# Transposing normed tokens by DMA instead of TensorE in a planned two-layer kernel

## Chip, cores, metric

One core of a Trainium2 chip.

## The reference, cut

Two layers, each a memory-augmented recurrent transformer block followed by a gated feed-forward network (FFN). 2048 tokens, width 512, 32 heads of 128, segments of 32 tokens with 8 memory tokens carried from one segment to the next.

```python
for s in range(n_seg):                          # 64 segments, in sequence
    h = concat([mem, x[:, s*32:(s+1)*32]], 1)   # 8 + 32 tokens
    q, k, v = h@Wq, h@Wk, h@Wv                  # 32 heads of 128
    p = softmax(where(mask, q@k.T * scale, -1e9))
    o = (p @ v) @ Wo
    mem = o[:, :8]; outs.append(o[:, 8:])
x = x + A(layernorm(x)); x = x + B(layernorm(x))   # B: sigmoid(x@Wg) * (x@Wu) @ Wd
x = x + A(layernorm(x)); x = x + B(layernorm(x))
```

The chain through `mem` is what forbids doing the segments side by side. The kernel therefore runs the two layers interleaved, six steps apart, in 70 steps of one segment each.

## The kernel before

The kernel doesn't write its instructions in program order. It adds *tasks* with reads, writes and assumed durations to a planner. The planner simulates the engines 24 times, forwards and backwards, keeps the order with the shortest forecast, and then emits the instructions in that order. Each engine's order is fixed from then on.

```python
    LAT = {"PE": 205.0, "DVE": 110.0, "ACT": 128.0, "POOL": 40.0, "SP": 4000.0}
    TO_PE = 32.0
    WAIT = 65.0                       # ns that the planner adds to a VectorE/ScalarE task with several waits
...
    def plan(self, rounds=24):        # keeps the best of 24 forecasts
```

A block is four segments, 128 tokens. Its tokens are normalized into `xn` (128 tokens x 512 features) and transposed, four 128x128 squares, into a PSUM bank. From there they are copied to `hT`, where the projections read them:

```python
    def layernorm_T(self, xb, xkey, rw=slice(0, P)):
        ...
        xn = pl.buf(self.xnp)
        ...
        pl.add("DVE", 340, lambda: nc.vector.tensor_scalar(out=xn[rw, :], in0=xb, scalar1=ln[rw, 6:7], scalar2=ln[rw, 9:10], op0=ALU.subtract, op1=ALU.mult),
               r=xkeys + [lk], w=[xn])
        B = pl.buf(self.bank, "bg")
        ...
        def tr():
            for c in range(DC):
                nc.tensor.transpose(out=pst()[:, c, rw], in_=xn[rw, c * P:(c + 1) * P], identity=self.ident[rw, rw])

        pl.add("PE", DC * mm_ns(rw.stop - rw.start), tr, r=[xn], w=[B])
        return pst, B
```

`pre1(b)` does this for the tokens of a first-layer block, four steps before their use. `v_fill`/`ln_x` does it for blocks 6, 9, 12, 15 once more, for rows that fill up a value pass. Meanwhile GpSimd keeps loading FFN weights, 256 KB a load, over and over (219, 219 and 218 loads for the three matrices, by the page). `last_weights` loads those of the last FFN, from SyncE or GpSimd as the planner likes.

## Time and profile before

| | before |
|---|---|
| time, median of 4 | 1878.2 us (1876.1 to 1882.9; 1879.8 was the median of the 3 known when predicting) |
| span of the profiled run, granted clock | 1874.4 us, 0.997 |
| TensorE busy | 98% |
| DMA traffic | 273.8 MB, of which GpSimd's weight loads 181.9 MB |

The prediction below shows the profile's lines. The list of DMA queues (queue and kind: packets, MB, share of 16 engines):

```profile
q0 software_dynamic: 59184, 181.87, 33.3%
q1 hardware_dynamic: 73918, 85.92, 16.1%
q8 instruction: 323, 5.29, 1.2%
```

q0 holds GpSimd's weight loads, q1 what SyncE issues. q8 carries *instructions*: 323 packets of 16 KB. In the trace TensorE runs 82762 instructions (matmuls, weight loads and a few others), 323.3 times 256: from these counts I estimate one packet for 256 of them, at 64 bytes each. So TensorE's program itself arrives by DMA, on a queue that the page lists beside those of the data, with 1.2% of the span of the core's 16 DMA engines.

### The profile page before, as it was taken

How to read it: one execution, taken by the hardware profiler on the slowest of the kernel's cores; microseconds unless marked ns; L12 is line 12 of the kernel's file. 1: busy time of each engine (PE TensorE's matmuls, PEld its weight loads, DVE VectorE, ACT ScalarE, POOL GpSimd, SP SyncE). 2: the span in 40 equal slices, each digit the busy share in tenths (PEclk: the TensorE clock that was granted, in tenths of full speed). 3: DMA queues.
4: the chain of work that ended last, by engine and by line, in shares of the span. 5: the costliest groups of instructions: out<-in, count | busy, mean ns of one | idle time of the engine just before them, and what ended most of it. 6: DMA issues, size and time to landing. Idle time of an engine off the chain costs nothing.

```text
span 1874.4 us, 94356 instructions
## 1 busy us (share of the span) xinstructions
PE 1835.2 (98%) x41250; PEld 1579.0 (84%) x41250; DVE 1281.1 (68%) x4167; ACT 1137.5 (61%) x2690; POOL 576.2 (31%) x822
## 2 busy tenths in 40 slices
PE   7999899999999999999999999999999999999998
PEld 3578788888889898989889898989889898988787
DVE  5466567776777667776676677666777677766564
ACT  5655566666666666566666666666666666665553
POOL 5413012232423232333323333233323232323321
PEclk9999999999999999999999999999999999999999
DMA  9734234554645554555545544555545454555535
GB/s 353 249 99 114 77 86 119 152 155 128 182 125 152 150 142 122 153 151 148 166 121 148 157 142 132 140 153 151 160 126 155 125 155 127 147 144 151 152 90 143
DMA packets 133516, 273.83 MB, mean 146 GB/s; under 512 B 29254, under 2 KB 64846, under 8 KB 133102
## 3 DMA queue, kind: packets, MB, share of 16 engines
q0 software_dynamic: 59184, 181.87, 33.3%
q1 hardware_dynamic: 73918, 85.92, 16.1%
q8 instruction: 323, 5.29, 1.2%
q14 instruction: 91, 0.75, 0.1%
HBM read 222.04 MB, written 27.26 MB: 133 GB/s over the span
## 4 chain that ended last, share of the span: by engine, by line
PE 94%; DMA 1%; ACT 1%; DVE 1%; issue 1%; POOL 1%; SPq 0%; ACTq 0%; POOLq 0%; DVEq 0%
PE bank L707 32%; PE bank L808 16%; PE bank L907 11%; PE bank L570 9%; PE bank L678 7%; PE bank L931 5%; PE bank L721 5%; PE bank L780 4%; PE bank L791 4%; PE bank L540 1%; ACT otsb L999 1%; DMA vsb<-sst 0%; PE bank L875 0%; DMA wd<-in_B_w_down_dram 0%; DMA wv_sb<-in_A_Wv_dram 0%
## 5 line engine op out<-in xcount | busy, mean ns | idle before, releaser
L707 PE MATMUL bank<-hT,wq_sb 128*128 128x80 bf16 (+1 forms) x8960 | 625.8, 198 | 5.6 <-issue 2.7
L707 PE MATMUL bank<-hT,wk_sb 128*128 128x80 bf16 (+1 forms) x8960 | 624.3, 198 | 2.1 <-issue 2.1
L999 ACT CAST qku<-bank 128x480 bf16<-128x480 f32 (+3 forms) x770 | 394.0, 512 | 267.3 <-PE bank L707 256.1
L707 PEld LDWEIGHTS <-wq_sb 128*128 128x128 bf16 x8960 | 459.1, 100 | 31.3 <-issue 12.0
L707 PEld LDWEIGHTS <-wk_sb 128*128 128x128 bf16 x8960 | 451.7, 99 | 1.2 <-issue 1.2
L734 DVE TENSOR_TENSOR st<-bank,maskb 80x240 f32<-80x240 f32 (+1 forms) x732 | 268.8, 369 | 231.8 <-PE bank L721 225.0
L808 PE MATMUL bank<-otsb,wo_sb 128*128 128x80 bf16 (+1 forms) x8960 | 372.0, 198 | 6.1 <-ACT otsb L999 5.4
L808 PEld LDWEIGHTS <-wo_sb 128*128 128x128 bf16 x8960 | 339.5, 99 | 21.7 <-issue 9.4
L899 POOL DMA_DIRECT2D wg<-in_B_w_gate_dram x217 | 165.0, 760 | 501.2 <-PE bank L907 425.9
L999 ACT CAST otsb<-bank 128x480 bf16<-128x480 f32 (+3 forms) x420 | 200.6, 486 | 77.3 <-PE bank L791 61.9
L925 POOL DMA_DIRECT2D wd<-in_B_w_down_dram x217 | 153.7, 710 | 251.6 <-PE bank L791 99.5
L763 DVE TENSOR_TENSOR pb<-st,rz 80x480 bf16<-80x480 f32 x348 | 205.9, 592 | 3.5
L744 ACT ACTIVATE st<-st 80x240 f32<-80x240 f32 (+3 forms) x420 | 159.9, 382 | 67.0 <-DVE st L741 65.4
L999 ACT CAST ptsb<-bank 128x480 bf16<-128x480 f32 (+3 forms) x315 | 155.8, 501 | 65.6 <-PE bank L780 63.2
L530 POOL TENSOR_TENSOR lns<-lns,negh 128x1 f32<-128x1 f32 (+1 forms) x79 | 45.3, 576 | 451.1 <-DVE lns L529 336.7
L746 DVE TENSOR_REDUCE sm<-st 80x6 f32<-80x240 f32 (+3 forms) x420 | 151.8, 363 | 43.7 <-ACT st L744 41.8
L721 PE MATMUL bank<-qku 128*80 128x80 bf16 (+1 forms) x2240 | 177.4, 202 | 0.0
L907 PE MATMUL bank<-xnT,wg 128*128 128x128 bf16 (+2 forms) x1784 | 171.8, 219 | 1.9 <-DMA wd<-in_B_w_down_dram 1.3
L907 PE MATMUL bank<-xnT,wu 128*128 128x128 bf16 (+2 forms) x1784 | 171.2, 218 | 0.4 <-issue 0.4
L721 PEld LDWEIGHTS <-qku 128*80 128x80 bf16 (+1 forms) x2240 | 130.4, 117 | 44.5 <-issue 10.6
L900 POOL DMA_DIRECT2D wu<-in_B_w_up_dram x217 | 162.5, 749 | 4.6 <-PE bank L707 2.0
L741 DVE TENSOR_TENSOR st<-st,mx 80x240 f32<-80x240 f32 (+3 forms) x420 | 155.8, 371 | 3.9
(99 smaller groups left out, 2499.9 us busy)
## 6 DMA issues: line engine op xcount, KB each, us to landing
wg<-in_B_w_gate_dram POOLq DMA_DIRECT2D x219, 256.0 KB, 4.3
wd<-in_B_w_down_dram POOLq DMA_DIRECT2D x219, 256.0 KB, 5.3
wu<-in_B_w_up_dram POOLq DMA_DIRECT2D x218, 256.0 KB, 4.8
vsb<-scr SPq DMA_DIRECT2D x512, 48.0 KB
vsb<-sst SPq DMA_DIRECT2D x280, 64.0 KB
scr<-vst SPq DMA_DIRECT2D x128, 96.0 KB
wv_sb<-in_A_Wv_dram SPq DMA_DIRECT2D x4, 1024.0 KB
wq_sb<-in_A_Wq_dram SPq DMA_DIRECT2D x5, 768.0 KB
```

The costliest lines, as they stand in the source:

```text
L570: nc.tensor.matmul(B[:, :], lhsT=tile[:, c, :], rhs=self.wv[:, c, cs], start=(c == 0), stop=(c == DC - 1))
L707: nc.tensor.matmul(o_ap, lhsT=W[:, c, h * P:(h + 1) * P], rhs=mv(c), start=(c == 0), stop=(c == DC - 1))
L721: nc.tensor.matmul(s_all(SB)[pr, uh - h0 + i, :], lhsT=qku[:, i, 0, 0:ncol], rhs=qku[:, i, 1, 0:ncol], start=True, stop=True)
L734: pl.add("DVE", dve_ns(n, True), lambda gsz=gsz, hs=hs, st=st, SB=SB, pj_=pj_, npj_=npj_, mk=mk, idx=idx: nc.vector.tensor_tensor(out=st[p ...
L741: pl.add("DVE", dve_ns(n), lambda gsz=gsz, hs=hs, st=st, mx=mx: nc.vector.tensor_tensor(out=st[pr, hs], in0=st[pr, hs], in1=mx[pr, hs].uns ...
L744: pl.add("ACT", act_ns(n), lambda hs=hs, st=st: nc.scalar.activation(out=st[pr, hs], in_=st[pr, hs], func=ACTF.Exp, scale=self.scale), r=s ...
L763: nc.vector.tensor_tensor(out=o, in0=st[pr, hs].unsqueeze(1).to_broadcast([npart, 2, gsz, L]), in1=rz[pr, :, 0:gsz].unsqueeze(3).to_broadc ...
L808: nc.tensor.matmul(WB[:, c * ncol:(c + 1) * ncol], lhsT=self.wo[:, h, c * P:(c + 1) * P], rhs=otsb[:, hl, 0:ncol], start=(h == 0 and c == ...
L899: pl.add("POOL", 760, lambda wg=wg, fs=fs: nc.gpsimd.dma_start(out=wg[:], in_=self.wgv[:, :, fs]), r=[("wo", self.H - 1)], w=[gk] + bt, la ...
L900: pl.add("POOL", 760, lambda wu=wu, fs=fs: nc.gpsimd.dma_start(out=wu[:], in_=self.wuv[:, :, fs]), r=[("wo", self.H - 1)], w=[uk] + bt, la ...
L907: nc.tensor.matmul(gu[:, 2 * i + k, 0:n], lhsT=W[:, c, i * P:(i + 1) * P], rhs=xnT[:, c, rw], start=(c == 0), stop=(c == DC - 1))
L999: nc.scalar.copy(out=dst, in_=src)
```

## The change

Intent: take 18 of the 79 groups of transposes off TensorE, which is busy 98% of the time, and let the transposing DMA do them, as the DMA engines are about half busy outside the boot; and keep the last FFN's weight loads out of SyncE's queue. The diff, cut (the copies `write_hT_x` and `take_v` only learn to wait for a list of keys):

```diff
-    def layernorm_T(self, xb, xkey, rw=slice(0, P)):
+    def layernorm_T(self, xb, xkey, rw=slice(0, P), by_dma=False):
 ...
-        xn = pl.buf(self.xnp)
+        xn, xk = (self.xp, "xp") if by_dma else (pl.buf(self.xnp),) * 2
 ...
-               r=xkeys + [lk], w=[xn])
+               r=xkeys + [lk], w=[xk])
+        if by_dma:
+            q = self.nxt("xvt", 2)
+            tile_, keys = self.xvf[q], [("xvf", q, g) for g in range(4)]
+            pl.add("SP", 1250, lambda: nc.sync.dma_start_transpose(out=tile_[:, :, :], in_=xn[:, :]), r=[xk], w=keys, lat=5000.0).land = 4000.0
+            return (lambda: tile_[:, :, :]), keys
 ...
-        return self.layernorm_T(xb[:, :], key)
+        return self.layernorm_T(xb[:, :], key, by_dma=b not in self.boot_x)
 ...
-        pst, B = self.layernorm_T(xb[:], ("xs", i))
+        pst, B = self.layernorm_T(xb[:], ("xs", i), by_dma=b >= 2)
 ...
-                    pl.add(("SP", "POOL"), {"SP": 450, "POOL": 760}, lambda tl=tl, src=src: ("dma", tl[:, :, :], src), w=keys, lat=6000.0)
+                    pl.add("POOL", 760, lambda tl=tl, src=src: nc.gpsimd.dma_start(out=tl[:, :, :], in_=src), w=keys, lat=6000.0)
```

More of the change, by code (lines that the diff above doesn't have):

```diff
@@ L550, in write_hT_x @@
             pl.add(("ACT", "DVE"), copy_ns(4 * SEG, True), lambda dst=dst, i=i: (dst, pst()[:, :, i * SEG:(i + 1) * SEG]),
-                   r=[B], w=[("hT", s, j, "x")])
+                   r=B if isinstance(B, list) else [B], w=[("hT", s, j, "x")])
     def take_v(self, pst, B, j, tile, keys, c0, r0, n):
@@ L557, in take_v @@
         self.pl.add(("ACT", "DVE"), copy_ns(16 * n, True),
-                    lambda: (dst, fview(pst()[:, 0, off:off + 1], [(P, self.DC), (SEG, BLK), (1, n)])), r=[B], w=keys)
+                    lambda: (dst, fview(pst()[:, 0, off:off + 1], [(P, self.DC), (SEG, BLK), (1, n)])), r=B if isinstance(B, list) else [B], w=keys)
     def v_pass(self, tile, keys, pieces, boot=False):
```

## The prediction

In the paragraph before part one, 222 ns is the mean of one 128x128 transpose on TensorE (L540), and 0.75 and about 0.4 us are what the issue of a load takes on GpSimd and on SyncE.

> **What bounds the kernel now.** I read the first part of the page (busy time by engine), then the slices, then the busy time by stretch, and then the chain that ended last.
>
> ```profile
> PE 1835.2 (98%) x41250; PEld 1579.0 (84%) x41250; DVE 1281.1 (68%) x4167; ACT 1137.5 (61%) x2690; POOL 576.2 (31%) x822
> ...
> PE   7999899999999999999999999999999999999998
> ...
> DMA  9734234554645554555545544555545454555535
> ```
>
> TensorE is busy 1835.2 of 1874.4 us. VectorE, ScalarE and GpSimd have a third of their time or more free, and the DMA engines are about half busy outside the boot. The idle 39.2 us of TensorE are not spread evenly; the view by stretch shows where they are (columns: PE busy, weight loads, VectorE, ScalarE, GpSimd, granted clock, DMA share, GB/s):
>
> ```profile
> 0.00:47.00 47.00, 36.26 (x300) 17.95 (x301) 24.72 (x78) 23.62 (x50) 27.23 (x54) 1.00 1.00 353
> ...
> 188.00:400.00 212.00, 202.56 (x4549) 178.53 (x4546) 144.20 (x465) 128.78 (x292) 50.01 (x69) 0.98 0.41 116
> 400.00:800.00 400.00, 395.40 (x8911) 349.16 (x8908) 286.01 (x931) 249.89 (x580) 122.53 (x172) 1.00 0.50 143
> ...
> 1200.00:1600.00 400.00, 398.47 (x8991) 352.39 (x8991) 283.83 (x922) 252.56 (x579) 125.40 (x174) 1.00 0.51 144
> ...
> 1827.00:1875.00 48.00, 42.00 (x979) 33.40 (x976) 23.33 (x79) 18.08 (x58) 9.20 (x13) 0.96 0.50 143
> ```
>
> The boot loses 10.7 us to its loads, the stretch to 400 us 9.4, the end 6.0; from 400 to 1600 us only about 9.5 us are idle in 1200. So the time is the sum of TensorE's instructions, laid end to end in one fixed order, and an instruction taken from TensorE in the middle is worth what it displaces there. The chain says the same: 94% of it is PE.
>
> ```profile
> by line: PE bank L707 32.5%; PE bank L808 15.5%; PE bank L907 10.6%; PE bank L570 9.5%; PE bank L678 6.9%; PE bank L931 5.1%; PE bank L721 5.0%; PE bank L780 4.1%; PE bank L791 3.7%; issue 1.0%; PE bank L540 0.9%; ACT otsb L999 0.6%; DMA vs
> ```
>
> L540, the transposes of all normed tokens, has 0.9% of it: the whole item that the change draws on is 16.9 us.
>
> [...] The trace has 222 ns for one on TensorE, and pipelined four take 0.39 us from first start to last end[...]. No transposing DMA is in this trace. [...] The trace has that time: 0.75 us for a weight load on GpSimd, about 0.4 us on SyncE. [...] The copies from the transposed tile leave PSUM for SBUF; from PSUM one of 128x128 takes 217 ns on VectorE here.
>
> **Part one: fewer TensorE transposes.** First how many. The view by the tile xn has the normalizations by their source:
>
> ```profile
> L531 DVE TENSOR_SCALAR xn<-xs,lns x36: 395/412/415, 9.0 to 1762.9; 128x512 bf16<-128x512 bf16 x36
> L531 DVE TENSOR_SCALAR xn<-xa,lns x35: 371/403/416, 39.0 to 1863.3; 128x512 bf16<-128x512 bf16 x33, 96x512 bf16<-96x512 bf16 x1, 32x512 bf16<-32x512 bf16 x1
> L531 DVE TENSOR_SCALAR xn<-xp,lns x4: 411/412/414, 86.2 to 1038.9; 128x512 bf16<-128x512 bf16 x4
> ```
>
> With four more from boot sources there are 79 groups of four transposes. The code sends to DMA the first layer's blocks 2 to 15 (14 of the 36 from xs; the others are blocks 0 and 1, four boot blocks and 16 second-layer blocks) and the four blocks 6, 9, 12, 15 from xp: 18 groups, 72 TensorE instructions. Then what one group is worth:
>
> ```profile
> 402.61 0.59 PE L808 MATMUL bank<-otsb,wo_sb 128*128 128x80 bf16 x12
> 403.04 0.39 PE L540 MATMUL bank<-ident,xn 128*128 128x128 bf16 x4
> 403.27 1.02 PE L808 MATMUL bank<-otsb,wo_sb 128*128 128x80 bf16 x24
> ```
>
> The group spans 0.39 us, but the next instructions start 0.23 us after its first: it displaces 0.23 us. Five of the six groups that I looked at show 0.22 to 0.24; in one an unrelated wait followed. 18 x 0.23 = **4.1 us**. The chain agrees: 18/79 of 16.9 us is 3.9. The busy time (97 ns each, 72 x 97 = 7.0 us) would overstate it, since it counts tails that lie under the next matmul.
>
> Second, TensorE's own waits for these groups. Between 188 and 1780 us:
>
> ```profile
> PE bank L791 <- DMA vsb<-scr: 1.9, 1, 1.9
> PE bank L791 <- DMA vsb<-sst: 1.6, 1, 1.6
> PE bank L540 <- DVE xn L531: 1.6, 4, 0.6
> ```
>
> 1.6 us are waits of L540 for the normalized tile, over both kinds of groups (weight loads waited 2.6 us in the same places, which is not to be added). I credit **0.7 us**. The PSUM buffer and the one xn buffer that 18 groups no longer hold are worth nothing that this view shows.
>
> Third, what the DMA adds. One transpose moves 128x512 bf16, 131 KB; 18 are 2.4 MB against 273.8 MB: bandwidth is no matter. Duration: [...] the diff itself plans 1.25 us of SyncE and 5 us to landing. Is that hidden? A step with both layers takes 26.3 us (the 57 copies of memory tokens, L821, run from 222.8 to 1697.2 us: 1474.4/56). The code asks for a block four steps, some 105 us, before its first use, and tokens of a block go to slots that are free by then. So 5 us are hidden. The buffers xvf are idle after the boot, and two suffice for 18 uses in 1600 us. The in-place use of xp chains the loads of blocks 9, 12, 15 to the transpose before: some 10 us with 100 us of slack.
>
> What is not hidden is the company in SyncE's queue: the strips' way from sst into vsb is used within the same step. I estimate that such a load is exposed for 4 of a step's 26.3 us, so 18 transposes meet it 18 x 4/26.3 = 2.7 times, each for 1 to 2 us, half of it foreseen by the fixed order: **+2 us**. The copies out of SBUF instead of PSUM (up to 72 on VectorE or ScalarE) should be a little shorter on VectorE; neither engine is the bound: 0.
>
> **Part two: the last weights in GpSimd's ring.** 21 loads; before, SyncE issued 10 of them. In the last stretch:
>
> ```profile
> 1836.56 0.75 POOL L995 DMA_DIRECT2D wv_sb<-in_B_w_up_dram  x1 [1.02 <-PE bank L678]
> 1837.30 1.49 POOL L995 DMA_DIRECT2D wv_sb<-in_B_w_gate_dram  x2
> 1838.77 0.75 POOL L995 DMA_DIRECT2D wv_sb<-in_B_w_up_dram  x1
> ```
>
> The space in wv_sb comes free with the last strips at 1836.5; twelve loads in one ring take 12 x 0.75 = 9 us to 1845.5, plus their landing of 4.4 to 7.6 us (the page's rows for wv_sb) 1853, while the last FFN's matmuls run from 1853.2 on and take the weights in order. So the last ones arrive just in time: **0, at worst +2 us**. SyncE gains 10 x 0.4 us there, before the last strips.
>
> **Sum.** -4.1 - 0.7 + 2 + 0 = -2.8 us. On top comes that the order of all instructions is planned anew, and small luck goes both ways: the 9.5 us idle between 400 and 1600 us could shrink or double. As the transposes sat at step boundaries with other work (value passes, FFN) beside them, I lean slightly towards a gain and take -4: 1879.8 - 4 = **1876 us**.
>
> **Rivals.** (A) The transposing DMA is slow or holds up SyncE's queue: if each delays the loads behind it until TensorE stands for 2 us, 18 x 2 = 36 us and 1912 us. For it: [...] TensorE's order is fixed, so a late load stops everything. Against it: TensorE lost only 3.5 us to vsb loads in 1592 us, so they have slack, and 18 in 1600 us is rare. (B) The freed time is not kept: at a step's end TensorE waits for the copy of new memory tokens (L821), and a transpose taken away leaves a hole there. Then 1879 to 1880 us. Against it: TensorE waited only 1.3 us for L821 in 1592 us, so there is other filler. (C) The new plan packs the boot and the early steps better, whose 20 us of idle are the largest sum to be had: with a third of it, 1869 us. Against it: the boot blocks keep their TensorE transposes, and the first 47 us wait for loads (DMA share 1.00). (D) The last loads come late on GpSimd and the end grows by 3 to 5 us: 1880 us.
>
> **Range and chances.** The three runs before span 6.2 us; the planned order may move it by 5 us either way; A in small doses adds 10. So 1867 to 1887. More than 2% faster (below 1842) would need all idle time gone: 0.01. More than 2% slower (above 1917) needs A in full: 0.04. Within 2%: 0.95.
>
> **What would show it.** Right: 72 fewer L540 matmuls (316 to 244), TensorE's busy time down by 4 to 7 us, TensorE's idle time unchanged within 5 us, xvf written by 18 DMAs on SyncE, vsb waits of TensorE below 6 us. Wrong: PE waits for vsb or hT of tens of us (A), idle before L707 for L821 above 5 us (B), much less idle before 400 us (C), waits of L907 or L931 for wv_sb in the last 25 us (D).

## More of the kernel before

The metric is device time in microseconds (us), median over several executions. Kernels are compared with executions of the kernel before on the same chip in the same rounds. Where two changed kernels of different rounds are compared by their medians, keep in mind that the median of the kernel before lay between 1877.7 and 1880.0 us in these rounds.

## The result, and the profile after

| | before | after |
|---|---|---|
| time, median of 4 each | 1878.2 us | 1890.4 us (1888.9 to 1893.0) |
| ratio, 95% interval | | 1.0063 (1.0039 to 1.0087) |
| span and clock of the profiled run | 1874.4, 0.997 | 1887.8, 0.995 |

The change makes the kernel 12 us slower: "same" at 2%, as predicted, but 14 us above the predicted time and 3.4 us outside the range. A ratio here is the mean time of one kernel's fast runs over that of the other's in the same rounds, so it is not quite the ratio of the medians quoted. Where differences in us are taken from a ratio below, they are (ratio - 1) x 1878.

The page of the kernel after: busy time by engine, TensorE and clock by slice, and the chain by engine.

```profile
PE 1825.8 (97%) x40966; PEld 1577.4 (84%) x41178; DVE 1280.8 (68%) x4169; ACT 1147.6 (61%) x2688; POOL 584.0 (31%) x833
...
PEclk9998999999999999999999999999999999999999
...
PE 90%; DVE 3%; ACT 2%; issue 2%; DMA 1%; POOL 0%; SPq 0%; ACTq 0%; DVEq 0%; POOLq 0%
```

The weight loads went from 41250 to 41178: exactly the 72 transposes are gone. (This trace lacks 212 matmul records, so PE's 1825.8 us is some 10 us too low; the weight loads are complete.) Yet the span grew by 13.4 us. The clock shows a dip in the fourth slice, which was not there before, and the chain has less PE (94% before) and more of VectorE, ScalarE and "issue". By stretch, first as in the prediction, then around that slice, before and after (columns as there):

```profile
188.00:400.00 212.00, 200.65 (x4550) 176.08 (x4570) 143.34 (x466) 128.26 (x293) 50.12 (x69) 1.00 0.42 119
...
1200.00:1600.00 400.00, 394.39 (x8883) 350.51 (x8929) 283.20 (x924) 257.31 (x580) 125.19 (x173) 1.00 0.52 145
```

```profile
130.00:155.00 25.00, 23.91 (x705) 20.19 (x701) 16.61 (x53) 14.12 (x42) 4.61 (x7) 1.00 0.37 110
```

```profile
130.00:155.00 25.00, 19.21 (x526) 16.63 (x524) 13.01 (x43) 11.60 (x39) 3.03 (x5) 0.80 0.55 107
```

From 1200 to 1600 us, 62 fewer weight loads fit into the same 400 us (8929 for 8991): the loss is not at the start alone. In the 25 us from 130 us on TensorE does 524 weight loads in place of 701, at a mean clock of 0.80, while the DMA engines are *busier* (0.55 against 0.37) and move *less* (107 against 110 GB/s). Per step (I count from a step's first weight load of `wq` to the next's), step 3 takes 24.8 us in place of 17.8.

What does TensorE wait for? The view of waits (total us, times, longest), before and then after; L826 is the line that was L821:

```profile
PE bank L707 <- issue: 4.8, 5, 1.9
...
PE bank L791 <- DMA vsb<-sst: 1.9, 2, 1.6
PE bank L791 <- DMA vsb<-scr: 1.9, 1, 1.9
...
PE bank L707 <- DVE hT L821: 1.3, 4, 0.3
```

```profile
PE bank L712 <- issue: 9.2, 9, 4.2
...
PE bank L712 <- DVE hT L826: 5.0, 16, 0.3
...
PE bank L683 <- issue: 1.7, 3, 1.0
PE bank L796 <- DMA vsb<-sst: 1.6, 2, 1.4
```

Not for `vsb`, the tiles of the attention's values (3.8 before, 1.6 now): the wait that rival A named did not come. Two others grew: by 3.7 us the wait for the new memory tokens, L826, and by some 7 us, over all lines, "issue", time in which TensorE waits for nothing that the profile shows. The longest, 4.2 us, is in step 3. The timeline (start, us, engine, line; in brackets the idle time before):

```profile
139.23 0.23 PE L712 MATMUL bank<-hT,wq_sb 128*128 128x40 bf16 x3
143.69 0.21 PE L712 MATMUL bank<-hT,wq_sb 128*128 128x40 bf16 x1 [4.22 <-issue]
143.73 0.30 PE L712 MATMUL bank<-hT,wk_sb 128*128 128x40 bf16 x4
```

TensorE stops after the third of four matmuls that accumulate one result from tiles long at hand. No data can be what it waits for. In the trace the place is the 193rd instruction of a block of 256, and the packet of instructions on q8 that ended before it ran from 141.09 to 142.39 us; TensorE resumed 1.3 us later. The other stops put down to issue, in the thirteen traces without missing records, lie at the same place, the 193rd or 194th instruction of 256, and end 1.2 to 1.7 us after a packet of q8 has ended (one of the 108, in e14, 2.3 us). **TensorE stood because its next instructions had not arrived.** In the kernel before, a packet of instructions ends a median 3.7 us before that place is reached, and in a tenth of the blocks only 2.2 us: some 1 to 2.5 us of slack, where TensorE takes 5.8 us on average for 256 instructions (1874.4/323). From here on I call such a stop a fetch stall. The kernel before has seven of them, 5.3 us in all.

What held the packet up? The tile `xvf`, written by the new DMAs:

```profile
L1004 ACT COPY hT<-xvf x32: 282/298/330, 141.6 to 1508.3; 128x128 bf16<-128x128 bf16 x32
L1006 DVE COPY hT<-xvf x24: 177/186/470, 335.8 to 1516.6; 128x128 bf16<-128x128 bf16 x24
L536 SPq DMA_TRANSPOSE xvf<-xp x18: 1209/1237/2177, 123.8 to 1501.5; - x18
```

The trace has each DMA's packets (512 of 256 B for a transpose) and its landing. Landing means here the first of a DMA's 16 completion marks; the last comes later, for block 2's transpose below at 11.1 us, for an undisturbed one at 2.4. An undisturbed transpose moves its data in 0.8 us and lands 2.3 us after its issue; so does block 3's in the slice here. But eight of the 18 took 3.5 us or more, and that of block 2, issued at 130.5 us, 9.3 us: nine weight loads had been issued on GpSimd between 125.8 and 132.4 us. There are packets of 256 B that took 2.2 us and weight packets of 4 KB that took 3.8 us (the slowest weight packet of the kernel before took 1.5 us). The DMA view of 134 to 146 us, in 40 slices of 0.3 us:

```profile
DMA  9999996009130069007899997981000892002000
GB/s 279 312 273 275 116 97 29 15 28 87 35 58 15 29 38 184 15 24 225 225 383 205 191 205 184 198 164 27 14 7 20 187 218 46 0 0 55 0 0 0
```

From about 135.8 to 139.4 us the engines move 15 to 87 GB/s in all slices but one, though the transpose was outstanding (its last packet ended at 139.3). TensorE's next packet of instructions starts only at 141.1; that it was held up behind the transpose is a reading, which the experiments below test.

From 141.9 us, still within the stall, to 152.1 us the granted clock is halved. At this point I took the stall to cost twice: its own length, and a slow stretch after it. The traces don't bear that out as a rule. In the traces of before and after, the halvings that end before the trace does last 3.4 us (three, before) and 10.2 and 6.8 us (after). One in before starts at 239.7 us, in a stop of TensorE of 1.6 us; but in e2, an experiment below without any transposing DMA, one starts at 142.9 us after no pause over 0.13 us in the 6 us before. And e5, another one without, has the clock halved from 141.4 to 151.7 us after a fetch stall of 0.9 us:

```profile
130.00:155.00 25.00, 23.19 (x638) 20.04 (x638) 14.03 (x46) 11.89 (x37) 4.98 (x8) 0.80 0.38 112
```

TensorE's order in e5 is that of the kernel before up to here. Steps 3 and 4 take 3.1 us longer in it, 0.9 of them the stall: an estimate of some 2 us for 10 us of halved clock.

**Theory:** transposing DMAs that meet a burst of weight loads hold up the DMA engines and so TensorE's instruction fetch; the stalls and (so I thought) the halved clock are the loss. **Rival 1:** the new order of the instructions is slower by itself. **Rival 2:** every transposing DMA costs its share, wherever it lies. **Rival 3:** part two, the last weights, costs.

### The profile page after: what moved, and what is told of

It is laid out like the page before. It is cut to its first block, busy times and chain, and to the rows that moved or that the text cites.

```text
span 1887.8 us, 94019 instructions
## 1 busy us (share of the span) xinstructions
PE 1825.8 (97%) x40966; PEld 1577.4 (84%) x41178; DVE 1280.8 (68%) x4169; ACT 1147.6 (61%) x2688; POOL 584.0 (31%) x833
## 4 chain that ended last, share of the span: by engine, by line
PE 90%; DVE 3%; ACT 2%; issue 2%; DMA 1%; POOL 0%; SPq 0%; ACTq 0%; DVEq 0%; POOLq 0%
PE bank L712 31%; PE bank L813 16%; PE bank L912 11%; PE bank L575 9%; PE bank L683 6%; PE bank L726 5%; PE bank L785 4%; PE bank L796 4%; PE bank L936 4%; ACT otsb L1004 1%; PE bank L545 1%; DVE st L739 1%; ACT qku L1004 0%; DMA xp<-in_A_x_dram 0%; DVE pb L768 0%
## 5 line engine op out<-in xcount | busy, mean ns | idle before, releaser
L712 PE MATMUL bank<-hT,wq_sb 128*128 128x80 bf16 (+1 forms) x8960 | 624.4, 198 | 12.2 <-DVE hT L826 5.0
L712 PE MATMUL bank<-hT,wk_sb 128*128 128x80 bf16 (+1 forms) x8960 | 623.4, 198 | 4.4 <-issue 4.4
L712 PEld LDWEIGHTS <-wq_sb 128*128 128x128 bf16 x8960 | 458.9, 99 | 34.5 <-issue 14.2
L712 PEld LDWEIGHTS <-wk_sb 128*128 128x128 bf16 x8960 | 451.1, 99 | 5.5 <-issue 5.5
L1004 ACT CAST ptsb<-bank 128x480 bf16<-128x480 f32 (+3 forms) x325 | 160.5, 497 | 62.5 <-PE bank L785 59.7
```

The source lines that it names most:

```text
L712: nc.tensor.matmul(o_ap, lhsT=W[:, c, h * P:(h + 1) * P], rhs=mv(c), start=(c == 0), stop=(c == DC - 1))
L1004: nc.scalar.copy(out=dst, in_=src)
```

## The experiments

Sixteen kernels ran, all five rounds, all reported correct. (The stale-tile kernels below compute on old tokens in places; the comparison does not notice it, so "correct" says nothing there.) The planner is a program, and its forecast of the span can be computed for each kernel: 1831.3 us before, 1837.7 after. When the constant `WAIT` is varied from 50 to 81, the forecast scatters with a standard deviation of 6 us for both kernels, around 1836.6 and 1835.3. So even on paper the change is worth 1.3 us, less than the draw that the re-planned order is.

### Order or DMA?

```diff
# e2_after_nodma (after, same order; stale tiles, wrong on purpose)
-            pl.add("SP", 1250, lambda: nc.sync.dma_start_transpose(...), ...)
+            pl.add("SP", 1250, lambda: None, ...)
```

> The changed kernel in its own order, with all 18 transposing DMAs left out; the copies read stale tiles, so the result is wrong on purpose. Theory (two causes: the order, +6, and one stall of the DMA engines in step 3 of the boot, +7 to 8): 1882 to 1885, still 4 to 7 us slower than before, step 3 of 18 us instead of 24.8. Rival 1 (all is the DMA's doing): as fast as before or 4 us faster, 1874 to 1878. Rival 2 (all is the order's doing): 1889 to 1891.

1882.2 us (1880.5 to 1883.7), ratio 1.0018 (1.0006 to 1.0030), as the theory had it. The order alone, with 72 transposes fewer, is 3.4 us *slower* than before (rival 1 holds for that part). The DMAs cost the other 8.2 us. Its waits show the same line L826 as after, at the same 16 step starts (ten of them are every fourth step from 15 to 51):

```profile
PE bank L712 <- DVE hT L826: 5.0, 16, 0.3
```

```diff
# e1_before_r10 (before, another draw of the order)
-    def plan(self, rounds=24):
+    def plan(self, rounds=10):
```

> The kernel before, with nothing changed but the number of rounds in which its planner looks for an order (10 for 24); no transposing DMA in it. The planner's own forecast of its span goes from 1831.3 to 1841.0 us (for the changed kernel it is 1837.7). Theory (a good part of the loss is a worse drawn order, and the planner's forecast differences come out on the chip): 8 to 11 us slower than before, about 1888. Rival (the loss is the DMA's own, orders of such forecasts are worth the same): within 2 us of before.

1883.6 us (1879.4 to 1884.1), ratio 1.0023 (1.0011 to 1.0035): nothing changed but the draw, and 4.3 us are lost, between the theory's 8 to 11 and the rival's 2. The forecast had been 9.7 worse.

```diff
# e5_lw_only (before with part two alone)
-  pl.add(("SP", "POOL"), {"SP": 450, "POOL": 760}, ... ("dma", tl[:, :, :], src), ...)
+  pl.add("POOL", 760, ... nc.gpsimd.dma_start(out=tl[:, :, :], in_=src), ...)
```

> The kernel before with part two of the change alone: the last FFN weights are issued by GpSimd only. The planner's forecast is 1831.7 us (1831.3 before). Theory (part two is neutral): within 2 us of before, 1876 to 1880. Rival (the ring of GpSimd delivers the last weights late): 3 to 5 us slower, with waits of TensorE for wv_sb in the last 25 us.

1876.9 us, ratio 0.9992 (0.9977 to 1.0006): part two is neutral, rival 3 is out.

```diff
# e12_before_dblpetr (before, same order, the 18 groups of transposes done twice)
-            for c in range(DC):
+            for c in list(range(DC)) * (2 if dbl else 1):
```

> The kernel before, its order unchanged, with each of the 18 groups of TensorE transposes in question done twice (72 transposes more). This prices what the change takes away. Prediction's step: 18 x 0.23 = +4.1 us, 1882. Rival (tails hidden or the time filled by waits anyway): within 1.5 us of before.

1880.9 us, ratio 1.0018 (1.0003 to 1.0032), +3.4 us, with an interval of 0.6 to 6.0: it agrees with the price of the 18 groups in the prediction, 4.1 us, but doesn't exclude the rival's 1.5.

### What of a transposing DMA costs?

```diff
# e3_after_drop1 (after without block 2's DMA, the one that took 9.3 us)
-            lambda: nc.sync.dma_start_transpose(...)
+            lambda: None if nth == 1 else nc.sync.dma_start_transpose(...)
```

> The changed kernel in its own order, with one transposing DMA of 18 left out, that of block 2, which is the second to run (at 130.5 us of the trace); wrong on purpose. Theory (this one meets a burst of nine weight loads, stalls the DMA engines, so that TensorE's instructions come 4.2 us late and its clock is halved for 10 us): step 3 falls from 24.8 to about 18 us, and the total by 7 to 8 us, to 1882 to 1884, the same as with all 18 left out. Rival (the burst alone stalls, the transpose only suffers from it, or all 18 cost a little each): step 3 keeps 22 us or more, total 1889 to 1891.

1888.9 us (1886.8 to 1890.3), ratio 1.0053 (1.0041 to 1.0065). Step 3 fell from 24.8 to 18.7 us, as expected, but only 1.5 of the expected 7 us reached the end: this run's trace has fetch stalls of its own, of 0.6 to 1.7 us, in steps 1, 5, 11, 27, 35, 47 and 51. The loss is not that one place.

```diff
# e4_before_shadow (before, order unchanged, plus 15 transposing DMAs that nobody reads)
         nc.vector.tensor_scalar(out=xn[rw, :], in0=xb, ...)
+        if sh: nc.sync.dma_start_transpose(out=dst[:, :, :], in_=xb)
```

> The kernel before in its own order, TensorE's transposes kept; 15 transposing DMAs of the same size are issued besides by SyncE where blocks 4 to 15 (first layer) and 9, 12, 15 are normalized, into tiles that nobody reads. Theory (outside the boot burst such a DMA costs next to nothing): 0 to 2 us slower than before. Rival (each holds up SyncE's queue or the DMA engines, some 0.5 us apiece): 6 to 10 us slower.

1885.0 us (1877.4 to 1888.3), ratio 1.0030 (1.0013 to 1.0047), +5.6 us. My expectation of about nothing outside the boot failed: transposing DMAs cost 0.4 us each on average in the order of before too, where nobody waits for them. The six times scatter over 11 us.

```diff
# e8_after_plaincopy (after, a plain copy of the same bytes; wrong on purpose)
-  ... nc.sync.dma_start_transpose(out=tile_[:, :, :], in_=xn[:, :]) ...
+  ... nc.sync.dma_start(out=tile_[:, :, :], in_=xn[:, :].rearrange("p (c n) -> p c n", c=self.DC)) ...
```

> The changed kernel in its own order; each of the 18 transposing DMAs is replaced by a plain copy of the same 131 KB from and to the same tiles by the same queue (the result is not transposed: wrong on purpose). Theory ([...] packets of up to 3.8 us during such a transfer): most of the 8 us goes away, 1881 to 1885, like with no DMA at all (1882). Rival (any transfer of this size in this place costs it): 1888 to 1891, like the changed kernel.

1883.8 us (1880.8 to 1890.7), ratio 1.0031 (1.0016 to 1.0046), where the theory, that the transposing itself is what costs, expected it: by the medians 1.6 us above no DMA at all, 6.6 below the transpose. Most of the cost is that of transposing, not of 131 KB more.

### A better order, with and without the DMAs

```diff
# e6_before_w50 and e7_after_w50: another draw for both kernels
-    WAIT = 65.0
+    WAIT = 50.0
# e9_after_w50_nodma: e7 with lambda: None for the DMA
```

> The kernel before with one constant of its planner changed (WAIT, 50 for 65), which only draws another order; forecast 1827.4 us, 3.9 less than before. Theory (orders of a better forecast are faster, of which about half arrives, as the forecast loss of 9.7 in the first experiment gave 4 to 6): 1 to 4 us faster, 1874 to 1877. Rival (forecast and time are not tied): same or slower.

1875.8 us (1873.8 to 1881.6), ratio 0.9989 (0.9974 to 1.0003): where the theory expected it, but the interval includes no change, so the rival isn't out. The profiled execution, the slowest of the five (1881.6), is worth a look. There is no such DMA in this kernel, and yet its view of waits has nine fetch stalls, 10.6 us:

```profile
PE bank L707 <- issue: 8.7, 8, 2.3
...
PE bank L721 <- issue: 1.9, 1, 1.9
```

So a fetch stall needs no transposing DMA, and one execution can have more of them than the median. What the DMAs add has to be read from medians, or from pairs of kernels in one order.

> The changed kernel with the same constant changed (50 for 65); forecast 1824.4 us, 13.3 less than the changed kernel's 1837.7. All 18 transposing DMAs are in it. Theory (order and DMA are two separate costs, about 4 and 8 us): the order's cost turns into a gain of some 3, the DMAs' 8 stay, so 1881 to 1885. Rival (the order is all that matters): 1871 to 1876, faster than before.

1889.5 us (1888.8 to 1891.5), ratio 1.0059 (1.0046 to 1.0072): an order forecast 13 us better than after's gained 1 us. Both theory and rival were missed. Block 2's DMA landed after 8.3 us, TensorE had a fetch stall of 3.4 us in step 3 again.

> The changed kernel planned with WAIT = 50 (the order of the run after_w50, 1889.5 us), its 18 transposing DMAs left out (stale tiles, wrong values on purpose). Theory (what the DMAs cost through TensorE's instruction fetch and the clock hid a better order in after_w50): step 3 falls back below 20 us and the time to 1874 to 1881, 8 to 15 us under after_w50. Rival (the order is at fault, forecasts of the planner are worth nothing here): 1885 or more, within 4 us of after_w50.

1874.8 us (1872.7 to 1876.8), ratio 0.9980 (0.9965 to 0.9994). The same order without its DMAs is 14.7 us faster than e7, and the fastest so far. The better order had been there; the DMAs ate it. Step by step, e7 and e9 take the same time within 0.3 us except in twelve of 69 steps. Nine of them, 3, 11, 19, 23, 31, 35, 43, 47 and 51, are exactly those in which e7's nine late transposes were on their way (47 is the one that is shorter, by 0.6 us, with its transpose); block 2's was issued 1.0 us after the start of step 3, each of the other eight 0.4 to 1.8 us before the start of its step. These nine steps hold 14.2 us of the difference; the other three are 5, 6 and 9. The steps with e7's quick transposes alone, 14, 26, 38 and 55, don't differ.

### Where a transpose lies

First try, by moving them all: the planner is told that a transpose takes longer to land, so that it issues it earlier.

```diff
# e10_after_w50_lat20 (WAIT = 50); e11_after_lat25 has lat=25000.0 and WAIT = 65
-  ... w=keys, lat=5000.0).land = 4000.0
+  ... w=keys, lat=20000.0).land = 4000.0
```

> Remedy: the changed kernel with WAIT = 50 and the latency that the planner assumes for a transposing DMA set from 5 to 20 us, so that it is issued some 13 to 15 us earlier, before the burst of weight loads on GpSimd's queue and not inside it; the planner forecasts 1818.1 us (before 1831.3, after 1837.7). Theory (collision with the weight burst is what makes a transposing DMA dear): nearly all transposes land within 3 us, block 2's too, step 3 below 20 us, fetch stalls down to 6 to 10 us, time 1870 to 1878, at least 10 us under after_w50. Rival (each transposing DMA costs its 0.4 to 0.5 us wherever it lies): 1882 or more.

1884.9 us (1882.3 to 1891.8), ratio 1.0040 (1.0022 to 1.0058).

> The same remedy with WAIT as it was (65) and 25 us of assumed latency; the planner forecasts 1821.1 us. Theory: most transposes land within 3 us, time 1872 to 1880. Rival: 1882 or more.

1892.0 us (1886.8 to 1898.1), ratio 1.0073 (1.0055 to 1.0091). Both remedies failed, by their rival's numbers. But their premise was not met: in e10 only five of 18 transposes landed within 3 us (the slowest after 8.9), in e11 three (10.6). GpSimd's traffic has few quiet places, and the earlier time was not one. So these two runs don't decide between "each costs" and "those that collide cost".

This does: the order of e7, to the instruction, with only half of the DMAs issued. In e7's trace nine landed within 3.5 us of issue and nine took 5.5 to 9.2 us. What they met tells them apart as well: between 6 us before and 1 us after the issue of a slow one GpSimd issued 6 to 10 DMAs, and packets of 672 to 778 KB on its queue started within the 3 us after it; for a quick one it issued 0 to 2, and at most 107 KB started (397 for the last).

```diff
# e13_after_w50_quick9 (e7; the other DMAs left out, stale tiles); e14_after_w50_slow9 is the complement
-  lambda: nc.sync.dma_start_transpose(...)
+  lambda: nc.sync.dma_start_transpose(...) if self.nxt("nth", 99) in (0, 2, 4, 5, 8, 9, 12, 13, 17) else None
```

> after_w50 (1889.5 us) with only those 9 of its 18 transposing DMAs issued that landed within 3.5 us there (the 1st, 3rd, 5th, 6th, 9th, 10th, 13th, 14th, 18th in time); the other 9 are left out (stale tiles, wrong values on purpose). The order is the same to the instruction as in after_w50 and after_w50_nodma (1874.8). Theory (only a transposing DMA that meets the burst of weight loads costs): 1874 to 1878. Rival (each costs its 0.8 us wherever it lies): 1881 to 1883.

1873.4 us (1871.4 to 1874.0), ratio 0.9965 (0.9949 to 0.9981).

> The complement: after_w50 with only the 9 transposing DMAs that took 5.5 to 9.2 us to land (the 2nd, 4th, 7th, 8th, 11th, 12th, 15th, 16th, 17th). Theory (collision with the weight loads is what costs): 1886 to 1891, nearly all of the 14.7 us. Rival (each costs the same): 1881 to 1883.

1886.3 us (1878.7 to 1895.2), ratio 1.0035 (1.0012 to 1.0059).

**The quick nine cost nothing, the slow nine 12.9 us**, though both are the same instruction with the same bytes in the same order of everything else. Rival 2 is out. The view of waits, of e13 and then of e14:

```profile
PE bank L912 <- issue: 1.1, 1, 1.1
...
PE bank L813 <- issue: 0.6, 1, 0.6
PE bank L712 <- issue: 0.5, 1, 0.5
```

```profile
PE bank L712 <- issue: 10.4, 8, 2.5
...
PE bank L683 <- issue: 1.9, 1, 1.9
...
PE bank L796 <- issue: 1.3, 1, 1.3
PE bank L813 <- issue: 1.3, 1, 1.3
PE bank L726 <- issue: 1.1, 1, 1.1
```

2.2 us of such waits with the quick half, 16.0 with the slow half (12 waits over 0.15 us, in 322 blocks of 256 instructions): the difference, 13.8 us, is about the whole loss (12.9 us by the medians, 14.3 between the two profiled executions). Little is left for the clock, which is halved for 13.7 us in e13 and for 17.1 in e14. Both traces have all their matmul records. In e14 the slow nine landed after 5.5 to 9.3 us again, in e13 the quick nine within 3.3.

### A correct version from it

```diff
# e15_mixed_w50 (after with WAIT = 50; by DMA only the groups that were quick)
-    ... by_dma=b >= 2)
+    ... by_dma=b in (3, 5, 8, 11, 15))
# e16_mixed7_w50: by_dma=b in (5, 8, 11)
# (both keep the four groups of blocks 6, 9, 12, 15 from xp on the DMA)
```

> A correct version drawn from the last two runs: the changed kernel with WAIT = 50, by DMA only the nine groups whose transposes landed quickly (blocks 6, 9, 12, 15 of the second tile and blocks 3, 5, 8, 11, 15 of the first), the other nine back on TensorE; planned anew, forecast 1824.4 us. Theory: the nine land within 3.5 us again and cost nothing, time 1871 to 1877, at or a little under before with WAIT = 50 (1875.8). Rival (the re-planned order brings them into the bursts again, or its draw is bad): 1880 or more.

1881.1 us (1876.5 to 1883.9), ratio 1.0008 (0.9991 to 1.0025), above the 1871 to 1877 expected. Planned anew, two of the nine fell into the bursts: block 3's took 9.0 us to land, and step 3 is back at 24.4 us, with the clock at 0.75:

```profile
130.00:155.00 25.00, 19.97 (x541) 17.43 (x538) 11.64 (x40) 10.96 (x35) 3.26 (x5) 0.75 0.54 124
```

Without these two:

> mixed_w50 without its two transposing DMAs that landed late (8.98 and 8.26 us; blocks 3 and 15 of the first tile), which go back to TensorE: seven by DMA, planned anew, forecast 1830.5 us. The five orders measured so far without late transposes ran 44 to 50 us over their forecast, the ones with late transposes 53 to 71. Theory: all seven land within 3.5 us, step 3 below 20 us, time 1874 to 1881. Rival (any transposing DMA costs, or something else is slow in these orders): over 1883, that is 53 or more over the forecast.

1877.1 us (1874.2 to 1880.9), ratio 0.9993 (0.9979 to 1.0006): in the expected range. Six of the seven landed within 2.7 us, one after 4.0, step 3 took 20.4 us, and no `issue` wait on L712 exceeds 0.9 us (one of 2.2 us is elsewhere). A correct kernel with transposing DMAs at the right places is as fast as before. It is not faster, and it isn't meant to beat e6, which has none at all.

### All runs beside their forecast

Both columns are us against the kernel before; the second is the planner's, the third from the measured ratio.

| kernel | forecast | measured |
|---|---|---|
| *no transposing DMA, or only quick ones* | | |
| e9 after, WAIT 50, none | -6.9 | -3.8 |
| e13 after, WAIT 50, quick nine | -6.9 | -6.6 |
| e6 before, WAIT 50 | -3.9 | -2.1 |
| e16 seven by DMA | -0.8 | -1.3 |
| e5 part two alone | +0.4 | -1.5 |
| e2 after, none | +6.4 | +3.4 |
| e1 before, 10 rounds | +9.7 | +4.3 |
| *with late ones* | | |
| e15 nine by DMA, two late | -6.9 | +1.5 |
| e14 after, WAIT 50, slow nine | -6.9 | +6.6 |
| e7 after, WAIT 50 | -6.9 | +11.1 |
| e10 issued earlier | -13.2 | +7.5 |
| e11 issued earlier | -10.2 | +13.7 |
| after | +6.4 | +11.8 |
| e4 before with 15 unread ones | 0 | +5.6 |
| e3 after without one | +6.4 | +10.0 |

(e8 and e12, with other work added, are left out.) In the upper half the measured differences follow the forecast, mostly at about half its size. In the lower half all lie 3.6 to 24 us above it: the planner knows nothing of instructions that arrive late.

## Why the prediction was wrong

Step by step, as the prediction had it:

1. **"18 groups", 72 instructions: right.** L540's 316 transposes became L545's 244. **"18 x 0.23 = 4.1 us": agrees** with e12 (+3.4 us), whose interval of 0.6 to 6.0 is wide.
2. **Part two, "0, at worst +2": right** (e5). Rival D is out.
3. **"5 us are hidden": right.** TensorE never waited for a transposed `xvf`, though a landing took up to 9.3 us. By the medians the copies became shorter on VectorE (215 ns from PSUM, 186 from `xvf`) and longer on ScalarE (272 and 298), without effect.
4. **"Bandwidth is no matter", and "what is not hidden is the company in SyncE's queue: +2 us": this step failed.** The 4 us of exposure and the 1 to 2 us a meeting were estimates of mine that no trace had shown. The company that mattered is not in SyncE's queue and not a tile: it is GpSimd's weight bursts on one side and TensorE's own instruction packets on the other. The term measured 8.2 us in after's order (after against e2) and 14.7 in another (e7 against e9). I had read DMA cost as bytes, landing and order within a queue, and never asked whether TensorE's program shares the DMA engines, though the page listed that queue.
5. **The re-planned order, "small luck goes both ways ... I lean slightly towards a gain": this failed too.** e2 is 3.4 us slower with 72 instructions fewer, so the new order by itself cost 7 to 8 us, more than the 4.1 freed: 3.7 of them as 12 more waits at step starts for the new memory tokens. That is rival B by its name, and at its mark of 5 us; but rival B had not allowed for a draw that takes more than was freed. Whether the removed transposes opened these holes or the draw did is not shown; e16, also with fewer transposes, has 6 such waits. The planner's forecast, which I had not computed, said +6.4.

The sum then reads: -4.1 freed, about +7.5 for the order, about +8.2 for the DMAs: +11.6, against 11.8 measured. (The 7.5 is what makes the first two add up to e2, so the sum is an account and no test.) The prediction was off by 14.4 us: 6.2 too little for the DMAs, about 9.4 for the order (the lean to a gain and the 0.7 us of waits included), less 1.6 by which the median of the kernel before itself moved between the two sets of runs; 0.4 us stay over, as medians and ratios are mixed. Rival A had the right sum of "a transfer disturbs others until TensorE stands", but the wrong victim, and a per-transfer size, 2 us, that only the late half comes near (12.9 us for nine).

**What stays open.** *That* late transposes come with late instruction packets is shown; *how* they block the DMA engines (why they move so little from 136 to 139 us with work outstanding) is not, nor what else causes fetch stalls, as in e6. What halves the clock around step 3 is open too: from 130 to 155 us it is 0.80 in e5 and e16 as well, without a late transpose. In e14 the quick half is missing and 3.2 us of e7's loss with it, within the intervals of both.

## What to carry to other kernels

TensorE, bound by its instructions here, also depended on their delivery (16.0 us of fetch stalls in e14, 5.3 in before). When a busy engine stops in the middle of an accumulation, waiting for nothing that the profile shows, count its instructions from the start, see whether the stops lie at one place of the count (here the 193rd or 194th of 256), and look at when the instruction queue's packets end (here 1.2 to 1.7 us before TensorE went on). Before moving work from a bound engine to a DMA "with time to spare", ask what bursts it meets, and test it with half of the transfers issued in an unchanged order: that separated a cost of 13 us from one of nothing. And where an order is re-planned by a search, a gain smaller than the spread of its draws (6 us here) can't be seen in one draw; compare kernels at equal order, or compute the forecast first.
